# Seven quarter products in place of eight in the second feed-forward layer of a fused attention kernel

## The chip, the cores and the metric

The kernel runs on one core of a Trainium2 chip. The metric is the device time of one execution in microseconds (us), as the median of three runs. The core's engines work side by side, each through its own list of instructions in a fixed order, and wait for each other by semaphores. TensorE (PE in the profile) multiplies matrices into PSUM, eight banks of 128 x 512 float32. Its weight loads (PEld) overlap its matmuls. VectorE (DVE) and ScalarE (ACT) do elementwise work, GpSimd (POOL) sets up constants, and SyncE (SP) issues the DMA transfers between DRAM and SBUF.

## The reference

Attention over 4 batches, 8 heads, 576 tokens and width 64 gives `x` of 2304 tokens x 512. Two feed-forward layers follow, and the second one is what changes:

```python
# layer 1
h = x @ w_in                       # 2304 x 512 @ 512 x 2048
g = s * maximum(h, 0) ** 2 + b
x = g @ w_out                      # 2304 x 2048 @ 2048 x 512
# layer 2, with weights of its own
h = x @ w_in2
g = maximum(h, 0) + alpha * minimum(h, 0)
out = g @ w_out2
```

## The kernel before

**Precision.** Each operand of a large product is split into a high part, rounded to the type fp32r, and a low part, the difference. A product is then three matmuls: high by high, high by low and low by high. The weights arrive as 64-bit words and are put together from two 32-bit halves by three VectorE instructions (L870, L873, L876), then split by a cast (L879) and a difference (L882).

**Tiling.** Values lie transposed: features on the 128 partitions, tokens along the columns. Layer 1 runs over one block of 512 tokens and seven of 256, layer 2 over four of 512 and one of 256 (`BLOCKS`). In each block a loop over 16 slices `f` of the hidden width makes one step: `g1` runs the first product (4 slices of the input, 12 matmuls, L932 to L934) into a bank, ScalarE and VectorE make the hidden values from it and split them (in layer 1 relu L946, square L947, cast L954, difference L955; in layer 2 L949, L952, L954, L955), and `g2`, one step later, adds the second product (4 slices of the output, 12 matmuls, L973 to L975) into four banks. `evac` then copies the banks out (ScalarE L1003 or L1006, VectorE L1008 or L1012) and stores them, layer 1's to the DRAM tensor `y1`, layer 2's to the output. `load_x` loads a block of input and splits it (L1044 and L1046 in layer 1, L1051 and L1053 in layer 2).

**Order.** `op` records every instruction with its engine, an assumed duration, what it reads and writes, and a priority (a lower number goes first; without one, the place in the program). `Plan.order` then simulates all engines once, at build time, and writes out each engine's instructions in the order found. It includes SP's list of DMAs. At run time nothing is reordered: an instruction that waits holds up whatever is behind it on its engine. Temporary buffers are 19 slots of 640 columns, 12 in `pool` and 7 in `poolx`. A `Slot` takes a place when the plan reaches its first instruction, if as many places as its reserve (`RES`) stay free; `claim` closes places for good. The attention of all four batches comes first in priority, layer 1 fills in behind it, and layer 2's weights (`weights`, loaded by L867) are loaded and split from the attention's end on, most of them in layer 1's last block. The input of layer 1 goes through the DRAM tensor `x1` (stored by L833, loaded by L1035).

## Time and profile before

| | us |
|---|---|
| median of three runs | 980.5 |
| lowest and highest of them | 980.23, 982.16 |
| the profiled execution, its own time | 980.97 |
| its span in the profile, first to last instruction | 978.9 |

The profile is of one execution, taken by the hardware. Busy time is the time in which an engine had an instruction running. Matmuls are pipelined, so a row's duration is longer than the spacing of two matmuls, and the spacing has to be read from starts. A row of a group of instructions names line, engine, operation, output and inputs by their tiles, shape and count, then busy time in us, the mean duration of one in ns, and the engine's idle time just ahead of them with what ended it. A timeline row gives start and duration in us. The granted clock is the share of TensorE's full rate, 2.4 GHz, that it was given.

### The profile page before, as it was taken

Reading aid. Unit: us, or ns where it says so; the run is one execution under the profiler, and the core shown is the slowest. Engines: PE = TensorE matmul, PEld = TensorE weight load, DVE = VectorE, ACT = ScalarE, POOL = GpSimd, SP = SyncE. Lnnn points to the kernel's source line nnn. Section 1 sums busy time; section 2 is a strip of 40 time slices with the busy share of each in tenths; the row PEclk is TensorE's granted clock in tenths of the full one; section 3 lists DMA queues with packets and bytes.
Section 4 is the critical chain, followed back from the end, with each engine's and each line's share of the span. In section 5 each row is a group of like instructions: output and inputs, shape, how many; then the busy total and the mean of one; then the engine's idle time right before and its main releaser. Section 6 shows DMA issues by size and latency. Waiting matters only on the chain.

```text
span 978.9 us, 18001 instructions
## 1 busy us (share of the span) xinstructions
PE 962.6 (98%) x7068; PEld 828.7 (85%) x7068; DVE 602.4 (62%) x1471; ACT 471.5 (48%) x1183; POOL 5.3 (1%) x29
## 2 busy tenths in 40 slices
PE   7999999999999999999999999999999999999998
PEld 5777777788888888999999998888888888888898
DVE  7999998677776766542122999945434443534344
ACT  7877766787787777645454663212112111211111
POOL 1000000000000000000000000000000000000000
PEclk9999999999999999999999999999999999999999
DMA  5359955465657555641000755502000200100010
GB/s 176 100 161 239 243 197 155 111 163 115 151 117 155 137 121 104 120 164 55 1 23 10 224 170 158 162 1 86 1 1 11 65 1 1 44 1 0 1 45 22
DMA packets 114693, 93.22 MB, mean 95 GB/s; under 512 B 83377, under 2 KB 94641, under 8 KB 114609
## 3 DMA queue, kind: packets, MB, share of 16 engines
q1 hardware_dynamic: 114608, 92.08, 34.8%
q8 instruction: 55, 0.90, 0.4%
q14 instruction: 30, 0.24, 0.1%
HBM read 59.29 MB, written 13.11 MB: 74 GB/s over the span
## 4 chain that ended last, share of the span: by engine, by line
PE 89%; DVE 5%; ACT 4%; issue 1%; DMA 0%; SPq 0%; ACTq 0%; DVEq 0%
PE yb L973 13%; PE yb L975 13%; PE yb L974 13%; PE hb L932 9%; PE hb L934 8%; PE hb L933 8%; PE sp L932 3%; PE sp L934 3%; PE sp L933 3%; PE ob L775 2%; PE ob L932 2%; PE ob L934 2%; PE ob L933 2%; PE sp L775 2%; PE yb L775 2%; PE sp L679 1%
## 5 line engine op out<-in xcount | busy, mean ns | idle before, releaser
L973 PE MATMUL yb<-gr,wt 128*128 128x256 f32 (+2 forms) x832 | 270.7, 325 | 0.7 <-ACT gr L954 0.5
L975 PE MATMUL yb<-gr,wt 128*128 128x256 f32 (+2 forms) x832 | 268.3, 322 | 0.0
L974 PE MATMUL yb<-gr,wt 128*128 128x256 f32 (+2 forms) x832 | 267.6, 322 | 0.0
L932 PE MATMUL hb<-xr,wt 128*128 128x256 f32 (+1 forms) x592 | 183.9, 311 | 5.3 <-ACT gt L946 3.7
L934 PE MATMUL hb<-xr,wt 128*128 128x256 f32 (+1 forms) x592 | 179.1, 303 | 0.3 <-DVE wt L882 0.3
L933 PE MATMUL hb<-xr,wt 128*128 128x256 f32 (+1 forms) x592 | 179.1, 303 | 0.0
L973 PEld LDWEIGHTS yb<-gr,wt 128*128 128x128 f32 x832 | 156.4, 188 | 17.1 <-issue 2.5
L975 PEld LDWEIGHTS yb<-gr,wt 128*128 128x128 f32 x832 | 157.1, 189 | 13.9 <-DVE gr L955 1.1
L974 PEld LDWEIGHTS yb<-gr,wt 128*128 128x128 f32 x832 | 156.5, 188 | 12.2
L955 DVE TENSOR_TENSOR gr<-gt,gr 128x256 fp32r<-128x256 f32 (+1 forms) x168 | 84.1, 501 | 126.8 <-ACT gr L954 126.4
L954 ACT CAST gr<-gt 128x256 fp32r<-128x256 f32 (+1 forms) x168 | 78.7, 468 | 143.3 <-DVE gt L952 136.1
L932 PEld LDWEIGHTS hb<-xr,wt 128*128 128x128 f32 x592 | 111.3, 188 | 18.2 <-ACT gt L946 6.1
L934 PEld LDWEIGHTS hb<-xr,wt 128*128 128x128 f32 x592 | 111.8, 189 | 5.8 <-DVE wt L882 0.7
L933 PEld LDWEIGHTS hb<-xr,wt 128*128 128x128 f32 x592 | 111.3, 188 | 4.5
L946 ACT ACTIVATE gt<-hb 128x256 f32<-128x256 f32 (+1 forms) x128 | 52.6, 411 | 98.2 <-PE hb L934 94.1
L954 ACT CAST gr<-mz 128x512 fp32r<-128x512 f32 (+1 forms) x40 | 23.2, 579 | 154.0 <-DVE mz L952 153.9
L932 PE MATMUL sp<-xr,wt 128*128 128x512 f32 (+1 forms) x160 | 58.8, 367 | 0.0
L933 PE MATMUL sp<-xr,wt 128*128 128x512 f32 (+1 forms) x160 | 58.8, 367 | 0.0
L934 PE MATMUL sp<-xr,wt 128*128 128x512 f32 (+1 forms) x160 | 58.8, 367 | 0.0
L947 ACT ACTIVATE gt<-gt 128x256 f32<-128x256 f32 (+1 forms) x128 | 57.1, 446 | 2.5
L955 DVE TENSOR_TENSOR gr<-mz,gr 128x512 fp32r<-128x512 f32 (+1 forms) x40 | 25.6, 639 | 25.1 <-ACT gr L954 25.1
L949 DVE TENSOR_SCALAR mz<-ob,alv 128x512 f32<-128x512 f32 (+1 forms) x20 | 14.0, 698 | 37.8 <-PE ob L934 37.6
(343 smaller groups left out, 1484.7 us busy)
## 6 DMA issues: line engine op xcount, KB each, us to landing
pool<-wout SPq DMA_DIRECT2D x18, 512.0 KB, 4.3
pool<-win SPq DMA_DIRECT2D x16, 512.0 KB, 4.1
room<-wout SPq DMA_DIRECT2D x14, 512.0 KB, 3.9
room<-win SPq DMA_DIRECT2D x13, 512.0 KB, 4.2
pool<-y SPq DMA_DIRECT2D x18, 256.0 KB, 4.4
out_t<-pool SPq DMA_DIRECT2D x16, 256.0 KB, 2.1
y<-pool SPq DMA_DIRECT2D x22, 128.0 KB, 1.8
pool<-kp SPq DMA_DIRECT2D x9, 288.0 KB, 4.0
```

The costliest lines, as they stand in the source:

```text
L775: T.matmul(bank_at(bk)[rows, x:x + n], half(sqp, odd, q0, nq), half(sk, odd, k0, n), start=True, stop=True, skip_group_check=True)
L932: T.matmul(H_, W_h, X_h, start=(d == 0), stop=False)
L933: T.matmul(H_, W_h, X_l, start=False, stop=False)
L934: T.matmul(H_, W_l, X_h, start=False, stop=(d == KD - 1))
L946: op("ACT", t_act(n, 50), lambda: A.activation(out=t_, in_=H_, func=AF.Relu), r=[hk, "gr"], w=[tk], prio=-1)
L947: op("ACT", t_act(n), lambda: A.activation(out=t_, in_=t_, func=AF.Square), w=[tk], prio=-1)
L949: op("DVE", t_dve(n, 1.04, 60), lambda: V.tensor_scalar(out=t_, in0=H_, scalar1=0.0, scalar2=alv[:, f:f + 1], op0=ALU.min, op1=ALU.mult), ...
L954: op("ACT", t_act(n), lambda: A.copy(out=G_h, in_=t_), r=[tk], w=[("gh", gj)], prio=-1)
L955: op("DVE", t_dve(n), lambda: V.tensor_tensor(out=G_l, in0=t_, in1=G_h.bitcast(F32), op=ALU.subtract), r=[tk, ("gh", gj)], w=[("gl", gj)], ...
L973: T.matmul(Y, W_h, G_h, start=first, stop=False, skip_group_check=True)
L974: T.matmul(Y, W_l, G_h, start=False, stop=False, skip_group_check=True)
L975: T.matmul(Y, W_h, G_l, start=False, stop=False, skip_group_check=True)
```

## The change

Layer 1 stays as it is, except for where its tiles lie. Layer 2 no longer goes through `g1` and `g2`. Its input, its two weight matrices and its hidden values are each taken as 2 x 2 quarters (tokens by 1152, input width by 256, hidden width by 1024), and each product is made of seven products of sums and differences of quarters, numbered 1 to 7, whose results are added up to the four quarters of the output.

`prepare` loads the four quarters of a slice of layer 2's weights, puts the words together, forms the four sums and differences that the scheme needs, and stores all seven pieces in the DRAM tensors `wd`. `fetch` brings them back and splits them, into the places of layer 1's weights. `inputs` loads the input's quarters for 384 tokens of each half, adds layer 1's bias, and forms and splits the operands `XP` of the seven products. `hidden` runs the first product in 24 groups (3 passes over tokens by 8 slices of the hidden width), seven `product` calls of six matmuls each. Product 4 is run one group late. Partial results are kept in PSUM or copied out (`copy_out`), added up (`join`), put through the leaky relu (`leak`), and the hidden values are stored in the DRAM tensor `g1`. `output` loads them back by quarters, forms and splits operands in a ring of three buffers, runs the second product in 3 passes of seven products of four steps with 12 matmuls each, and stores the sums. All these matmuls have 384 columns.

```diff
-BLOCKS = {1: [(0, 512)] + [(t, 256) for t in range(512, NT, 256)],
-          2: [(t, min(512, NT - t)) for t in range(0, NT, 512)]}
+BLOCKS = [(0, 512)] + [(t, 256) for t in range(512, NT, 256)]
 NBIG, NB = 512, 256
+NS, NTH = 384, NT // 2
+GATE = 8
+GROUPS = [(b, f) for b in range(NTH // NS) for f in range(8)]
...
 def t_b(n):
...
         sb.tile([128, 16], F32, name="lead")
@@ -333,21 +341,29 @@
...
-            if layer == 1 and blk == len(BLOCKS[1]) - 1:
-                weights(win2, wout2, f, 2)
+            if blk == len(BLOCKS) - 1 and f % 2:
+                fetch("wi", f // 2)
...
+        PLACE = {1: (0, 0), 2: (0, 1), 5: (0, 2), 6: (0, 3), 3: (1, 0), 7: (1, 1), 4: (1, 2)}
...
+        def prepare(src, key, i):
...
+            fa, fb = Slot(RES["pf"], size=2), Slot(RES["pf"], size=2)
...
+            for x, f in enumerate((fa, fb)):
+                s = Slot(RES["pw"], size=2)
+                op("SP", 475, lambda s=s, x=x: nc.sync.dma_start(out=at(s, 1024, I32), in_=src[i, x]),
+                   r=[("x1", B - 1, NP - 1, 1), "words"], w=[s], bytes_=524288)
...
+            for out, in0, in1 in (((fa, 512), (fb, 0), (fa, 0)), ((fa, 768), (fb, 256), (fa, 512)),
+                                  ((fb, 512), (fb, 256), (fb, 0)), ((fb, 768), (fa, 256), (fa, 768))):
+                op("DVE", t_dve(256), lambda out=out, in0=in0, in1=in1: V.tensor_tensor(
+                    out=q(*out), in0=q(*in0), in1=q(*in1), op=ALU.subtract), r=[fa, fb], w=[out[0]])
+            for x, (f, a, n) in enumerate(((fa, 0, 4), (fb, 256, 3))):
+                op("SP", 475, lambda f=f, a=a, x=x, n=n: nc.sync.dma_start(
+                    out=wd[key][:, i, x, 0:256 * n], in_=q(f, a, 256 * n)), r=[f], w=[("wd", key, i, x)], bytes_=131072 * n)
+        def fetch(key, i):
...
+            for x, a, n in ((1, 0, 3), (0, 0, 2), (0, 2, 2)):
+                f = 2 * i + x
+                if key == "wi":
+                    old = wkeys("wi", f) + wkeys("wo", f)
+                    s = Buf("poolx", 2 * GW + (1024 if x else 256 * a), 256 * n)
+                else:
+                    old = []
+                    s = Buf("poolx", 0, 768) if x else Buf(4 + a // 2, 0, 512)
...
+                act(s, 475, lambda s=s, x=x, a=a, n=n: nc.sync.dma_start(out=see(s), in_=wd[key][:, i, x, 256 * a:256 * (a + n)]),
+                    r=[("wd", key, i, x)], extra_w=old, bytes_=131072 * n, prio=-4, eng="SP")
+                op("ACT", t_act(256 * n), lambda s=s, x=x, a=a, n=n: A.copy(out=wp(i, x)[:, a:a + n, 0, :], in_=fold(see(s))),
+                   r=s.keys, w=[("w2", i, x, a)], prio=-0.8 if key == "wi" else -0.5)
+                op("DVE", t_dve(256 * n), lambda s=s, x=x, a=a, n=n: V.tensor_tensor(
+                    out=wp(i, x)[:, a:a + n, 1, :], in0=fold(see(s)), in1=wp(i, x)[:, a:a + n, 0, :].bitcast(F32), op=ALU.subtract),
+                   r=s.keys, w=[("w2", i, x, a)], prio=-0.8 if key == "wi" else -0.5)
...
+        every = [("wd", key, i, x) for key in ("wi", "wo") for i in range(8) for x in range(2)]
+        def act(buf, dur, fn, r=(), prio=None, eng="ACT", extra_w=(), bytes_=0):
+            claim, extra = hold(buf)
+            op(eng, dur, fn, r=list(r) + (every if claim else []) + ([("g2", GATE)] if buf in XP.values() else []) + (
+                [("y1", len(BLOCKS) - 1, d) for d in range(KD)] if claim and max(claim) > NSLOT - XS + 4 else []),
+               w=buf.keys + extra + list(extra_w), prio=prio, claim=claim, bytes_=bytes_)
+        XP = {P: Buf("poolr", 4 * NS * i, 4 * NS) for i, P in enumerate((5, 6, 3, 2, 4))}
+        XP.update({P: Buf("xr", 4 * NS * i, 4 * NS) for i, P in enumerate((1, 7))})
+        RAW = [Buf("spare", 2 * NS * i, 2 * NS) for i in range(4)]
+        SUM = Buf("poolx", 0, 2 * NS)
+        FREE = [Buf(i, 0, NS) for i in range(6)]
...
+        def split(src, dst, prio):
+            act(dst, t_act(2 * NS), lambda: A.copy(out=see(dst, F32R, 0, 2 * NS), in_=see(src)), r=src.keys, prio=prio)
+            op("DVE", t_dve(2 * NS), lambda: V.tensor_tensor(
+                out=see(dst, F32R, 2 * NS, 2 * NS), in0=see(src), in1=see(dst, F32, 0, 2 * NS), op=ALU.subtract),
+               r=src.keys, w=dst.keys, prio=prio)
+        def sub(out, a, b, prio, o=ALU.subtract):
+            act(out, t_dve(out.n), lambda: V.tensor_tensor(out=see(out), in0=see(a), in1=see(b), op=o),
+                r=a.keys + b.keys, prio=prio, eng="DVE")
+        def inputs(b):
...
+            soon = -3 if b else -0.7
+            for P in (1, 5, 6, 3, 2, 7):
+                if P == 5:
+                    sub(SUM, a21, a22, soon, ALU.add)
+                elif P == 6:
+                    sub(SUM, SUM, a11, soon)
+                elif P == 3:
+                    sub(SUM, a12, SUM, soon)
+                elif P == 7:
+                    sub(a21, a11, a21, soon)
+                split({1: a11, 2: a12, 7: a21}.get(P, SUM), XP[P], soon)
+        def product(P, g, bank):
+            b, f = GROUPS[g]
+            def mm():
+                for k in range(2):
+                    X_h, X_l = (see(XP[P], F32R, 2 * NS * lo + NS * k, NS) for lo in range(2))
+                    W_h, W_l = (weight(P, f, lo, k) for lo in range(2))
+                    o = bank_of[bank][:, 0:NS]
+                    T.matmul(o, W_h, X_h, start=(k == 0 and P in (1, 5, 2)), stop=False, skip_group_check=True)
+                    T.matmul(o, W_h, X_l, start=False, stop=False, skip_group_check=True)
+                    T.matmul(o, W_l, X_h, start=False, stop=False, skip_group_check=True)
+            op("PE", t_s(NS), mm, r=[ready(P, f)] + XP[P].keys, w=[bank] + [("end", P)] * (g + 1 == len(GROUPS)), prio=MOE + cm["m"])
+            cm["m"] += 1
+        def copy_out(bank, out):
+            act(out, t_act(NS, 50), lambda: A.copy(out=see(out), in_=bank_of[bank][:, 0:NS]), r=[bank], prio=-1)
+        def join(bank, part, out):
+            act(out, t_dve(NS), lambda: V.tensor_tensor(out=see(out), in0=bank_of[bank][:, 0:NS], in1=see(part), op=ALU.add),
+                r=[bank] + part.keys, prio=-1, eng="DVE")
...
+        def leak(g, q, src, bank, out):
+            b, f = GROUPS[g]
+            f += 8 * (q % 2)
+            n = pick(TEMP)
+            r = [bank] if bank else src.keys
+            see_ = (lambda: bank_of[bank][:, 0:NS]) if bank else (lambda: see(src))
+            act(n, t_act(NS, 50 if bank else 93), lambda: A.activation(out=see(n), in_=see_(), func=AF.Relu, scale=-1.0), r=r, prio=-1)
+            act(out, t_dve(NS, 1.04, 60), lambda: V.scalar_tensor_tensor(
+                out=see(out), in0=see(n), scalar=alm[:, f:f + 1], in1=see_(), op0=ALU.mult, op1=ALU.add),
+                r=r + n.keys + ["alm"], prio=-1, eng="DVE")
+            k, t0 = GROUPS[g][1], NS * b
+            op("SP", 475, lambda: nc.sync.dma_start(out=g1_[:, q, k, t0:t0 + NS], in_=see(out)), r=out.keys,
+               w=[("g", b, q, k)], bytes_=512 * NS)
+        def hidden():
...
+            inputs(0)
+            ng = len(GROUPS)
+            bk = lambda g: (("S0", "H", ("Y", 0))[g % 3], ("O", ("Y", 2))[g % 2], ("S1", ("Y", 1))[g % 2])
+            parts = {}
+            def last(g):
+                al = bk(g)[0]
+                product(4, g, al)
+                leak(g, 2, None, al, pick(RING))
+                if GROUPS[g][0] == NTH // NS - 1:
+                    fetch("wo", GROUPS[g][1])
+            for g, (b, f) in enumerate(GROUPS):
+                al, be, ga = bk(g)
+                p1, u2, p5 = (SIDE[3 * (g % 2) + x] for x in range(3))
+                product(1, g, al)
+                copy_out(al, p1)
+                product(5, g, ga)
+                copy_out(ga, p5)
+                if g > 0:
+                    last(g - 1)
+                if f == 0:
+                    split(RAW[3], XP[4], -3 if b else -0.7)
+                product(6, g, al)
+                copy_out(al, u2)
+                product(3, g, ga)
+                c = pick(RING)
+                join(ga, u2, c)
+                leak(g, 1, c, None, c)
+                product(2, g, be)
+                c = pick(RING)
+                join(be, p1, c)
+                leak(g, 0, c, None, c)
+                product(7, g, al)
+                c = pick(RING)
+                join(al, p5, c)
+                leak(g, 3, c, None, c)
+                if f == 7 and g + 1 < ng:
+                    inputs(b + 1)
+            last(ng - 1)
...
+        def output():
+            U = [quarter(q) for q in range(4)]
+            ring = [Buf("gr", 0, 4 * NS)] + [Buf("xr", 4 * NS * i, 4 * NS) for i in range(2)]
+            side = FREE + [Buf("poolx", 4 * NS + NS * i, NS) for i in range(7)] + SIDE[0:3]
...
+                t0 = NS * b
+                for q in (3, 2, 0, 1):
+                    for m in range(4):
+                        act(U[q][m], 475, lambda u=U[q][m], q=q, m=m, t0=t0: nc.sync.dma_start(
+                            out=see(u).rearrange("p (k n) -> p k n", k=2), in_=g1_[:, q, 2 * m:2 * m + 2, t0:t0 + NS]),
+                            r=[("g", b, q, 2 * m + e) for e in range(2)] + (
+                                [("end", P) for P in (5, 6, 3, 2, 4)] if U[q][m].region == "poolu" else []), eng="SP", bytes_=1024 * NS)
+                kept = {}
+                for P in (4, 5, 1, 2, 6, 3, 7):
+                    bank = names[{1: "a", 6: "a", 7: "a", 2: "b", 5: "c", 3: "c", 4: "d"}[P]]
+                    for m in range(4):
+                        a11, a12, a21, a22 = (U[q][m] for q in range(4))
+                        if P == 5:
+                            sub(a22, a21, a22, None, ALU.add)
+                        elif P == 6:
+                            sub(a22, a22, a11, None)
+                        elif P == 3:
+                            sub(a12, a12, a22, None)
+                        elif P == 7:
+                            sub(a21, a11, a21, None)
+                        src = {4: a22, 5: a22, 6: a22, 1: a11, 2: a12, 3: a12, 7: a21}[P]
+                        dst = ring[count[0] % len(ring)]
+                        count[0] += 1
+                        split(src, dst, None)
+                        def mm(P=P, m=m, dst=dst, bank=bank):
+                            for e in range(2):
+                                G_h, G_l = (see(dst, F32R, 2 * NS * lo + NS * e, NS) for lo in range(2))
+                                for j in range(2):
+                                    W_h, W_l = (weight(P, 2 * m + e, lo, j) for lo in range(2))
+                                    o = bank_of[bank[j]][:, 0:NS]
+                                    T.matmul(o, W_h, G_h, start=(m == e == 0 and P in (1, 2, 4, 5)), stop=False, skip_group_check=True)
+                                    T.matmul(o, W_l, G_h, start=False, stop=False, skip_group_check=True)
+                                    T.matmul(o, W_h, G_l, start=False, stop=False, skip_group_check=True)
+                        op("PE", 2 * t_s(NS), mm, r=[ready(P, 2 * m + e) for e in range(2)] + dst.keys, w=bank,
+                           prio=MOE + cm["m"])
+                        cm["m"] += 1
+                    for j in range(2):
+                        if P in (4, 5, 1, 6):
+                            kept[P, j] = buf()
+                            copy_out(bank[j], kept[P, j])
+                        else:
+                            for part, q in {2: ((1, 0),), 3: ((6, 1),), 7: ((4, 2), (5, 3))}[P]:
+                                c = buf()
+                                join(bank[j], kept[part, j], c)
+                                d, tq = j + 2 * (q % 2), t0 + NTH * (q // 2)
+                                op("SP", 475, lambda c=c, d=d, tq=tq: nc.sync.dma_start(out=outT[:, d, tq:tq + NS], in_=see(c)),
+                                   r=c.keys, bytes_=512 * NS)
-        for i, (layer, blk) in enumerate((l, j) for l in (1, 2) for j in range(len(BLOCKS[l]))):
-            moe(layer, blk, i % 2 if layer == 1 else 2 + blk % 2)
+        for key, src in (("wi", win2), ("wo", wout2)):
+            for i in range(8):
+                prepare(src, key, i)
+        for blk in range(len(BLOCKS)):
+            moe(blk, blk % 2)
         flush()
+        hidden()
+        output()
```

Left out of the diff are the buffers' bookkeeping (`Buf`, `see`, `hold`), the loads of the input with its bias, the places of the quarters in `output`, the new layout of the weights' array, and the lines of layer 1 that only lose their layer argument.

## Rows read from the trace of the kernel before

**Rows 1.** Page, busy time (share of the span) and instructions of each engine

```profile
PE 962.6 (98%) x7068; PEld 828.7 (85%) x7068; DVE 602.4 (62%) x1471; ACT 471.5 (48%) x1183; POOL 5.3 (1%) x29
```

**Rows 2.** Page, TensorE's busy tenths and granted clock in 40 slices of the span

```profile
PE   7999999999999999999999999999999999999998
PEclk9999999999999999999999999999999999999999
```

**Rows 3.** Windows: us; busy (count) of PE, PEld, DVE, ACT, POOL; clock, DMA share, GB/s

```profile
450.00:500.00 50.00, 50.00 (x438) 49.80 (x437) 10.50 (x26) 24.43 (x64) 0.00 (x0) 1.00 0.08 25
550.00:600.00 50.00, 50.00 (x353) 46.92 (x352) 47.86 (x88) 26.58 (x58) 0.00 (x0) 1.00 0.62 182
700.00:750.00 50.00, 50.00 (x222) 41.40 (x221) 19.21 (x27) 5.61 (x9) 0.00 (x0) 1.00 0.00 1
```

**Rows 4.** Timeline of VectorE, layer 2's 512-wide blocks: first and last of 25 L949

```profile
684.81 0.75 DVE L949 TENSOR_SCALAR mz<-ob,alv 128x512 f32<-128x512 f32 x1 [2.51 <-PE ob L934]
...
815.37 0.75 DVE L949 TENSOR_SCALAR mz<-ob,alv 128x512 f32<-128x512 f32 x1 [2.50 <-PE ob L934]
```

**Rows 5.** Timeline: first and last of 12 L955, 12 L955 (258 wide), 15 L949

```profile
458.83 0.43 DVE L955 TENSOR_TENSOR gr<-gt,gr 128x256 fp32r<-128x256 f32 x1 [2.29 <-ACT gr L954]
...
488.75 0.43 DVE L955 TENSOR_TENSOR gr<-gt,gr 128x256 fp32r<-128x256 f32 x1 [2.29 <-ACT gr L954]
...
503.04 0.43 DVE L955 TENSOR_TENSOR gr<-gt,gr 128x256 fp32r<-128x256 f32 x1 [2.39 <-ACT gr L954]
...
533.99 0.43 DVE L955 TENSOR_TENSOR gr<-gt,gr 128x256 fp32r<-128x256 f32 x1 [2.39 <-ACT gr L954]
...
932.43 0.48 DVE L949 TENSOR_SCALAR mz<-sp,alv 128x256 f32<-128x256 f32 x1 [0.72 <-PE sp L934]
...
972.01 0.49 DVE L949 TENSOR_SCALAR mz<-ob,alv 128x256 f32<-128x256 f32 x1 [0.91 <-PE ob L934]
```

**Rows 6.** Groups of instructions by line and form, the two widths of cast and difference

```profile
L955 DVE TENSOR_TENSOR gr<-gt,gr 128x256 fp32r<-128x256 f32 x120 | 50.9, 424 | 106.8 <-ACT gr L954 106.4
L954 ACT CAST gr<-gt 128x256 fp32r<-128x256 f32 x120 | 48.8, 406 | 19.5 <-DVE gt L952 16.9 <-PE yb L974 0.2
L955 DVE TENSOR_TENSOR gr<-gt,gr 128x512 fp32r<-128x512 f32 x48 | 33.2, 691 | 20.0 <-ACT gr L954 20.0
L954 ACT CAST gr<-gt 128x512 fp32r<-128x512 f32 x48 | 29.9, 623 | 123.8 <-DVE gt L952 119.1 <-PE yb L974 3.7 <-PE yb L975 1.0
```

**Rows 7.** Timeline of VectorE without gaps, 256 and 512 wide

```profile
546.69 0.42 DVE L955 TENSOR_TENSOR gr<-gt,gr 128x256 fp32r<-128x256 f32 x1
547.03 0.42 DVE L870 TENSOR_SCALAR pool<-pool 128x512 int32<-128x512 int32 x1
547.37 0.68 DVE L882 TENSOR_TENSOR wt<-pool,wt 128x512 fp32r<-128x512 f32 x1
547.97 0.68 DVE L873 SCALAR_TENSOR_TENSOR pool<-pool 128x512 int32<-128x512 int32 x1
```

**Rows 8.** Timeline of SP: last x1 store, weight loads, last y1 stores

```profile
422.26 0.32 SPq L833 DMA_DIRECT2D x<-pool  x1
...
425.37 0.41 SPq L867 DMA_DIRECT2D pool<-win  x1
425.87 0.38 SPq L867 DMA_DIRECT2D pool<-wout  x1
...
584.97 2.04 SPq L1014 DMA_DIRECT2D y<-pool  x4
```

**Rows 9.** DMA issues from 424.5 to 426.5: KB each, us from issue to landing

```profile
pool<-win SPq DMA_DIRECT2D x1, 512.0 KB, 4.0
pool<-wout SPq DMA_DIRECT2D x1, 512.0 KB, 5.2
```

**Rows 10.** Timeline of the end: last matmul, last copy out of a bank

```profile
975.13 0.28 PE L975 MATMUL yb<-gr,wt 128*128 128x256 f32 x1
...
975.44 0.43 DVE L1012 COPY pool<-yb 128x256 f32<-128x256 f32 x1 [0.25 <-PE yb L975]
```

More of the change, by code (lines that the diff above doesn't have):

```diff
@@ L978, in g2 @@
                    w=[yk, ("g2", f)] + ([(yslot[d], "y")] if d in yslot else []),
[L979 removed]
+                   prio=MOE + cm["m"] + (1.5 if n == NBIG else 0))
             cm["m"] += 1
@@ L1035, in load_x @@
                 op("SP", 475, lambda xr=xr, src=src: nc.sync.dma_start(out=xr(), in_=src), r=rk,
-                   w=[s] + [("xset", x) for x in ((0, 1, 3) if xs == 3 else (xs,))], bytes_=512 * step * n,
-                   prio=-2 if layer == 2 and blk > 0 else None)
+                   w=[s, ("xset", xs)], bytes_=512 * step * n)
                 for e in range(step):
@@ new lines, in ready, with weight, __init__ @@
+        def ready(P, i):
+            x, a = PLACE[P]
+            return ("w2", i, x, 0 if x else a // 2 * 2)
+        def weight(P, i, lo, k):
+            x, a = PLACE[P]
+            return wp(i, x)[:, a, lo, k * 128:(k + 1) * 128]
+        class Buf:
+            def __init__(self, region, c0, n):
+                self.region, self.c0, self.n = region, c0, n
+                key = "pool" if region in ("poolr", "poolu") else region
+                self.keys = [(key, c) for c in range(c0 // 128, (c0 + n + 127) // 128)]
@@ new lines, in build, with hold @@
+        seen = set()
+        def hold(buf):
+            claim, extra = [], []
+            for k in buf.keys:
+                if k in seen:
+                    continue
+                seen.add(k)
+                region, c = k
+                lo, hi = 128 * c, 128 * c + 127
+                if region == "pool":
+                    claim += range(NSLOT - XS)
+                elif region == "poolx":
+                    o = NSLOT - XS
+                    claim += range(o + lo // GW, o + hi // GW + 1)
+                elif region == "xr":
+                    extra += [("xset", int(hi >= 2 * KD * NB))]
+                elif isinstance(region, int):
+                    extra += wkeys("wi", 2 * region + 1) + wkeys("wo", 2 * region + 1)
+                elif region in ("gr", "gt"):
+                    extra += [(x, j) for x in (("gh", "gl") if region == "gr" else ("gt",)) for j in range(2)]
+            return sorted(set(claim)), list(dict.fromkeys(extra))
```

260 lines of the change are left out of this document (142 added, 118 removed).

## The prediction

> **What bounds the kernel now.** I read the busy times first, then the slices of the span, then the stages in windows, and last the rows from which one instruction is priced. TensorE is busy 962.6 of 978.9 us, the next engine 602.4 [rows 1]; its busy digit is 9 from the second of the forty slices to the last but one [rows 2]. In the windows of layer 1 and layer 2 it is busy for the whole 50 us, with VectorE at 10 to 20 us of 50, except where layer 2's weights are decoded, 47.86 of 50 [rows 3]. So what layer 2 costs is its matmuls times their spacing, and only taking matmul time away, or adding waits, moves the end.
>
> The spacing has to be read from a marker that comes once in each step of 24 matmuls (12 of the first product, 12 of the second), because a busy matmul row overlaps its neighbours and some records are missing. In the 512-wide blocks 24 steps lie between 684.81 and 815.37 [rows 4]: 5.44 us a step, 226.7 ns a matmul. In the 256-wide block at the end 14 steps take 39.58 us [rows 5]: 2.827 us, 117.8 ns. Layer 2 is therefore 4 x 16 x 5.44 + 16 x 2.827 = 348.2 + 45.2 = 393.4 us, nothing idle in it. Layer 1's 256-wide blocks give 2.72 us (11 steps in 29.92), 113.3 ns, and the block with 258 columns in its second product 2.814 us (11 steps in 30.95): with 113.3 ns for its 12 matmuls of 256 columns, the 258-wide ones take 121 ns [rows 5].
>
> **The change: what leaves TensorE.** Seven quarter products in place of eight. First product: 24 groups x 7 x 6 = 1008 matmuls; second: 3 passes x 7 x 4 x 12 = 1008; all 384 wide, 2016 of them in place of 1536 of 512 and 384 of 256. No row has 384 columns. In cycles of 2.4 GHz (the granted clock is 1.00 throughout, its upper level [rows 2]) 256 columns cost 272, 258 cost 291 and 512 cost 544: 16 over the columns at 256, 32 or 33 above. So I take 384 + 32 = 416, 173.3 ns. The bounds are the ratio of the clean rows, 17/16, 170.0 ns, and that of the slower last block, 117.8 x 1.5 = 176.7 ns. Then 2016 x 173.3 = 349.4 us (342.7 to 356.2), and TensorE loses 393.4 - 349.4 = 44.0 us (37.2 to 50.7). Instructions grow from 1920 to 2016, so not the whole eighth comes back.
>
> The Trainium skill, TensorE: Matmul & The Clock Gate, section "Wait — 56ns, not 53.3ns?", puts a warm stream at the columns over 2.4 plus about 2.5 ns, 215.7 ns measured at 512. The rows say 226.7 ns [rows 4] and decide. By the page, as an estimate, layer 2 would be 373.4 before and 327.6 after, 45.8 us less.
>
> **What is added beside TensorE, and its cover.** The prices: a VectorE instruction on 256 columns starts 0.34 us before the next, one on 512 columns 0.60 [rows 7]; along that line 384 columns are 0.47 and 768 are 0.86 (the profile's durations, 424 and 691 ns, contain a tail under the next instruction [rows 6]). ScalarE casts take 406 and 623 ns [rows 6], so 0.51 and 0.84.
> - First product, per group of 42 matmuls = 7.28 us: VectorE three joins and four leaks, 7 x 0.47 = 3.3 us; ScalarE three copies and four relus, 3.6 us. Covered. Each value TensorE waits for (a copy out of a bank before the next product adds to it) has two other products, 2.08 us, between, against 0.51 plus handing over.
> - A new pass over 384 tokens: 11 more VectorE instructions of 0.86 (9.5 us) and ScalarE 7 x 0.84 + 8 x 0.51 = 10.0 us, within about two groups (14.6 us) that hold 6.6 already: 16.1 in 14.6. The operands are single buffers, each free only after its last product in group 7 and wanted one group later. TensorE waits 0 to 4 us there; I take 1.0 for each of two.
> - Second product, per pass 28 x 12 x 173.3 = 58.2 us: VectorE 44 x 0.86 + 8 x 0.47 = 41.6, ScalarE 28 x 0.84 + 8 x 0.51 = 27.6. The products 6, 3 and 7 are the dense part: 12 steps of 1.72 plus two joins, 21.6 in 25 us. Covered by a ring of three buffers, 0 to 2 us a pass; I take 0.5 x 3.
> - Weights: decoding them was 32 x (0.34 + 3 x 0.60) = 68.5 us of VectorE; now 32 x 1.54 + 64 x 0.34 = 71.1 us, moved ahead to the time after the attention, and 16 x (0.86 + 2 x 0.60) = 33.0 us for fetching and splitting again, half of it in layer 1's last block, half in the last pass of the first product. VectorE has the room: 10.5 of 50 us in layer 1's middle [rows 3].
>
> **Waits that the change adds.** (1) The loads of one pair of weight pieces wait until the pair before is decoded. Behind them on SP stand layer 1's stores and loads; behind each decode that waits for its load stands, on VectorE, the low part of the hidden values, for which the next second product waits. Two such loads issued 0.5 us apart landed after 4.0 and 5.2 us [rows 8, 9], so the second is there at 5.7; decoding 1.54 and handing over make 7.5 us a pair, 16 pairs 120 us. The attention's last store is issued at 422.3 and the first load then at 425.4 [rows 8]: done near 546, the last pieces stored near 551. The operand buffers in the pool want all of them, and step 8 of layer 1's last block, seven steps of 2.827 before the last stores at 585.0 [rows 8], near 565. So 14 us of slack. VectorE's order is fixed ahead, so loads later than planned can hold TensorE: 0 to 10 us, I take 1.5. (2) Layer 2's first operands can be split only after step 8: 6 splits and 4 differences of 0.86, four weight fetches of 2.06 and layer 1's own 7 x 0.34 are 19.2 us of VectorE in the 20 that are left, but product 1 needs only the first split: 0 to 8 us, I take 2.0. (3) Between the two products, the loads of three of the four quarters wait for the last product 4, whose operands stood in their place. Only product 4 (four steps of 2.08 = 8.3 us) runs without them. A load of 0.39 MB lands 4.0 us after issue and each next one 1.3 later (0.39/0.52 of the 1.7 us between the two landings above); sum, cast and difference take 2.6: 6.6 us, just within the cover; 0 to 7, I take 1.0. (4) At the end four joins follow the last matmul where four copies, two of them on ScalarE, did: the last one started 0.31 us after the last matmul's start [rows 10]. Two joins more in VectorE's row are 0.94 us, of which a half-step is hidden: 0.5 (0 to 1.5).
>
> Sum of the waits: 2 x 1.0 + 1.5 + 1.5 + 2.0 + 1.0 + 0.5 = 8.5 us. The profiled execution took 980.97 us, 2.07 over its span, and the median of the runs is 980.5, 0.5 lower: 980.97 - 44.0 + 8.5 = 945.5, and 945.0 for a median.
>
> **Rivals.**
> - Spacing at the ratio 17/16 and next to no waits: 980.5 - 50.7 + 1 = 931. For it: both clean rows have that ratio. Against: 258 columns already pay what 512 pay [rows 5].
> - Layer 2 starts late or layer 1 is paced by weight loads: the two upper bounds, 10 and 8 for 3.5, give 945 + 14.5 = 959.5. For: both engines' rows in that block come to nine tenths of it. Against: the 14 us of slack.
> - The second product is paced by its chain: if the difference of the next step isn't run under the cast, a step takes 0.86 + 0.84 + 0.86 = 2.56 where TensorE wants 2.08; 48 steps (four products of four, three passes) x 0.48 = 23 us, 968; with handing over of 0.25 each, 980, no change. Against: the ring holds three steps and the order is planned ahead.
> - Slower: the pool gives no room for two pairs of weights in flight, so each pair also waits for the stores of the one before: 5.7 + 1.54 + four differences of 0.34 + 4.0 for the stores, with handing over about 13 us, 16 pairs 208 us, until 633; layer 2 can run only product 1 before, 48 us after layer 1's end: 993 to 1001. It decides from 10 us a pair on. For: the stores use the same queue. Against: a pair wants 8 of 19 slots.
> - Slower: the clock falls at each new wait. One group at half the rate costs 7.28 us more; at six places (start, two passes, the boundary, two passes) 44 us, 989. Against: the granted clock is 1.00 in all forty slices although TensorE idled 16 us of the span [rows 1, 2]. The same page of the Trainium skill, section "HAM oscillation — how this bites in real kernels", says that idling brings the lower level back; no run here shows it.
>
> **How the numbers follow.** Forecast, 933 to 955 (the small waits at their ends and the spacing between its bounds): 0.66. Close spacing, 925 to 933: 0.08. Late start, 955 to 966: 0.11. Chain in the second product: 0.07, of which 0.02 at no change. Weights too slow: 0.06. Clock: 0.02. From 931 to 966 lies about 0.83. Faster by over 0.2% (2 us, what a measurement of this kernel can tell): 0.66 + 0.08 + 0.11 + 0.05 = 0.90; same 0.02; slower 0.08.
>
> **What would show it.** Right: markers of the first product's groups 7.2 to 7.4 us apart and steps of the second near 2.08; TensorE busy to the end with idle time of some 8 us after 420, at the four places named; granted clock 1.00. Wrong: groups of 7.5 us or more (spacing), decodes that wait for loads with TensorE's gaps right behind (weights), TensorE waiting for VectorE in products 6, 3 and 7 (chain), or a gap of several microseconds between the two products (the quarters' loads).

## The result, and the profile after

The changed kernel takes 955.5 us (median of four runs, 954.75 to 957.7) against 980.9 for the kernel before (four runs as well): a ratio of 0.9743, 95% interval 0.9723 to 0.9763, 25.5 us less. Forecast were 945.0, between 931 and 966, faster with 0.9. The direction and the range hold; of the 36 us that were expected to remain, 10 are missing. All rows of after in this section are from a run of 957.7 us with a span of 955.8.

Page, busy time of each engine, and TensorE's busy tenths and granted clock in 40 slices, to be read beside [rows 1, 2]:

```profile
PE 926.7 (97%) x7164; PEld 849.3 (89%) x7164; DVE 720.9 (75%) x1638; ACT 605.4 (63%) x1411; POOL 5.4 (1%) x29
...
PE   7989999999999899999999999799999999999998
PEclk9899999999999999999999999899999999999999
```

TensorE still sets the time. Its instructions are 96 more, as counted ahead, and it is busy 36 us less. Two slices of the clock are now below 9, the second and the 26th (597 to 621 us), and in the latter the busy digit falls to 7 as well: that is layer 2's start. What the second slice costs is settled with e9. Windows of 100, 25 and 200 us (columns as in [rows 3]):

```profile
300.00:400.00 100.00, 96.95 (x1046) 84.70 (x1042) 67.83 (x219) 75.75 (x208) 1.03 (x5) 0.98 0.60 131
...
600.00:625.00 25.00, 17.91 (x79) 16.14 (x78) 17.11 (x29) 13.66 (x26) 0.00 (x0) 0.80 0.63 201
...
725.00:925.00 200.00, 200.00 (x1150) 198.98 (x1150) 162.12 (x216) 107.16 (x169) 0.00 (x0) 1.00 0.55 170
```

From 725 to 925, which holds the change from the first product to the second, no time is lost, while VectorE is busy four fifths of it. From 600 to 625, 79 matmuls stand where 144 would fit. Between 300 and 400, in the attention, 3 us are idle; before it was less than 1. The spacing of the new matmuls, timeline of TensorE, six steps from one row to the other:

```profile
589.50 0.33 PE L1233 MATMUL ob<-poolr,wp 128*128 128x384 f32 x1
...
590.54 0.33 PE L1233 MATMUL sp<-xr,wp 128*128 128x384 f32 x1
```

1.04 us for six is 173.3 ns, 416 cycles of 2.4 GHz: the forecast's value. What TensorE waits for (waits by engine and line: us in total, times, longest) has entries that the kernel before has not:

```profile
PE sp L1233 <- DVE poolx L1260: 5.6, 1, 5.6
...
PE hb L925 <- ACT xr L1018: 1.6, 1, 1.6
PE hb L1233 <- DVE poolx L1248: 1.2, 1, 1.2
```

The first of them, in the timelines of TensorE, ScalarE, VectorE and SP:

```profile
610.74 0.34 PE L1235 MATMUL ob<-poolr,wp 128*128 128x384 f32 x1
616.70 0.69 PE L1233 MATMUL sp<-xr,wp 128*128 128x384 f32 x1 [5.62 <-DVE poolx L1260]
617.19 0.52 PE L1234 MATMUL sp<-xr,wp 128*128 128x384 f32 x1
617.51 0.52 PE L1235 MATMUL sp<-xr,wp 128*128 128x384 f32 x1
...
612.70 0.83 ACT L1107 CAST wp<-poolx 128x768 fp32r<-128x768 f32 x1 [1.93 <-DMA poolx<-wdwi]
...
613.56 2.43 DVE L1109 TENSOR_TENSOR wp<-poolx,wp 128x768 fp32r<-128x768 f32 x3 [2.07 <-ACT wp L1107]
616.03 0.61 DVE L1260 SCALAR_TENSOR_TENSOR poolx<-poolx,alm,sp 128x384 f32<-128x384 f32 x1
...
609.26 6.45 SPq L1105 DMA_DIRECT2D poolx<-wdwi  x5
```

TensorE wants a PSUM bank (sp) for a new product 1. The bank is held by a finished product 4 until its leak (L1260) has read it, and the leak stands behind the weights' differences (L1109), which wait for their casts (L1107), which wait for the weights to land (L1105). Why a leak should come after the weights is in the plan of places: `RING`, the buffers for the leak's output, lies with four of its seven buffers on columns 1280 to 2816 of poolx, and `fetch` puts the weights on 1280 to 3072 of the same tile until the last slice is through.

Behind the wait the matmuls stand 0.32 us apart. The granted clock in three stretches:

```profile
612.00:616.00 4.00, 0.00 (x0) 0.00 (x0) 2.29 (x3) 2.07 (x3) 0.00 (x0) 0.89 0.56 147
616.00:624.00 8.00, 6.06 (x18) 5.55 (x19) 5.68 (x10) 3.94 (x8) 0.00 (x0) 0.50 0.28 104
624.00:626.00 2.00, 2.00 (x10) 2.00 (x9) 1.76 (x4) 1.83 (x5) 0.00 (x0) 0.66 0.92 331
```

It fell to 0.50, the 1.2 GHz level, while TensorE stood still, and was back about 9 us after the matmuls had begun again. The 65 matmuls that are missing from 600 to 625 are 65 x 0.1733 = 11.3 us; 7.1 of them are idle time (25.00 - 17.91), so some 4 us, by this estimate, are the slower spacing. The prediction could cite the Trainium skill's section "HAM oscillation — how this bites in real kernels" (TensorE: Matmul & The Clock Gate), that idling brings the lower level back, without a row for it; this trace agrees, 0.50 after 5.62 us.

In the attention, SP's rows (the last x1 store answers to [rows 8], where it is at 422.26 us) show a thing of layer 2 that is there early, two of its loads of y1:

```profile
185.40 2.04 SPq L1205 DMA_DIRECT2D spare<-y  x2
...
425.74 0.32 SPq L851 DMA_DIRECT2D x<-pool  x1
```

And the end, last matmul and the joins behind it, to be read beside [rows 10]:

```profile
950.84 0.34 PE L1365 MATMUL sp<-xr,wp 128*128 128x384 f32 x1
...
950.69 1.02 DVE L1248 TENSOR_TENSOR gr<-sp,waste 128x384 f32<-128x384 f32 x2 [4.07 <-PE sp L1365]
951.63 0.55 DVE L1248 TENSOR_TENSOR gt<-sp,waste 128x384 f32<-128x384 f32 x1
952.09 0.55 DVE L1248 TENSOR_TENSOR waste<-sp,waste 128x384 f32<-128x384 f32 x1
```

The span ends 4.96 us after the last matmul's start (955.8 - 950.84), before 3.77 (978.9 - 975.13).

The theory from this trace: 44 us came, as computed; about 9 went at layer 2's start (the wait, and the clock that fell with it), about 7 in the attention, whose work is in another order, and 1.2 at the end. The program makes the order of all engines' work with a planner, so an instruction that layer 2 adds can move others far ahead of it. The first such instruction in VectorE's list is a 90-ns operation (`alm` from `alv`, L1270), which needs only what is there from the start.

All runs, each against runs of the kernel before on the same chip:

| Kernel | us | ratio to before, 95% interval |
|---|---|---|
| after | 955.5 | 0.9743 (0.9723 to 0.9763) |
| e1: layer 2 kept out of the attention | 956.3 | 0.9757 (0.9741 to 0.9773) |
| e2: other buffers for the leak | 946.8 | 0.9651 (0.9628 to 0.9673) |
| e3: both | 940.6 | 0.9592 (0.9578 to 0.9606) |
| e4: before, one 90-ns operation more | 996.9 | 1.0170 (1.0155 to 1.0185) |
| e5: the wait filled with matmuls | 955.6 | 0.9737 (0.9716 to 0.9757) |
| e6: e3, product 3 last | 939.2 | 0.9574 (0.9558 to 0.9590) |
| e7: e4 without moving the weights | 981.9 | 1.0014 (1.0001 to 1.0026) |
| e8: e3, weights moved by 64 bytes | 950.8 | 0.9688 (0.9668 to 0.9708) |
| e9: e3, the operation free | 941.5 | 0.9590 (0.9574 to 0.9606) |
| e10: e3, the loads free | 950.7 | 0.9686 (0.9672 to 0.9700) |

### The profile page after: what moved, and what is told of

It is laid out like the page before. It is cut to its first block, busy times and chain, and to the rows that moved or that the text cites. A ratio compares the mean times of both kernels' runs of the same rounds, so it can differ in the third digit from the quotient of the medians.

```text
span 955.8 us, 19300 instructions
## 1 busy us (share of the span) xinstructions
PE 926.7 (97%) x7164; PEld 849.3 (89%) x7164; DVE 720.9 (75%) x1638; ACT 605.4 (63%) x1411; POOL 5.4 (1%) x29
## 4 chain that ended last, share of the span: by engine, by line
PE 88%; DVE 4%; ACT 4%; DMA 3%; issue 1%; SPq 0%; DVEq 0%
PE hb L925 7%; PE yb L959 7%; PE hb L926 7%; PE yb L961 7%; PE hb L927 7%; PE yb L960 6%; PE yb L1363 3%; PE yb L1365 3%; PE yb L1364 3%; PE sp L1363 3%; PE sp L1365 3%; PE sp L1364 3%; PE sp L793 2%; PE yb L1233 2%; PE yb L1235 2%; PE yb L1234 2%
## 5 line engine op out<-in xcount | busy, mean ns | idle before, releaser
L925 PE MATMUL hb<-xr,wt 128*128 128x256 f32 (+1 forms) x512 | 153.3, 299 | 4.5 <-ACT gt L938 2.8
L959 PE MATMUL yb<-gr,wt 128*128 128x256 f32 (+2 forms) x512 | 153.4, 300 | 0.5 <-ACT gr L940 0.5
L961 PE MATMUL yb<-gr,wt 128*128 128x256 f32 (+2 forms) x512 | 150.3, 293 | 0.4 <-DVE gr L941 0.4
L926 PE MATMUL hb<-xr,wt 128*128 128x256 f32 (+1 forms) x512 | 149.5, 292 | 0.2 <-DVE xr L1020 0.2
L927 PE MATMUL hb<-xr,wt 128*128 128x256 f32 (+1 forms) x512 | 149.4, 292 | 0.0
L925 PEld LDWEIGHTS hb<-xr,wt 128*128 128x128 f32 x512 | 96.6, 189 | 10.9 <-ACT gt L938 4.3
L959 PEld LDWEIGHTS yb<-gr,wt 128*128 128x128 f32 x512 | 96.5, 188 | 9.7 <-issue 5.9
L941 DVE TENSOR_TENSOR gr<-gt,gr 128x256 fp32r<-128x256 f32 (+1 forms) x128 | 58.4, 456 | 59.1 <-ACT gr L940 57.2
L961 PEld LDWEIGHTS yb<-gr,wt 128*128 128x128 f32 x512 | 96.4, 188 | 3.7 <-DVE gr L941 1.0
L927 PEld LDWEIGHTS hb<-xr,wt 128*128 128x128 f32 x512 | 96.4, 188 | 2.7
L926 PEld LDWEIGHTS hb<-xr,wt 128*128 128x128 f32 x512 | 96.4, 188 | 2.6 <-DVE xr L1020 0.4
L960 PE MATMUL yb<-gr,wt 128*128 128x256 f32 (+2 forms) x320 | 93.5, 292 | 0.0
L960 PEld LDWEIGHTS yb<-gr,wt 128*128 128x128 f32 x320 | 60.2, 188 | 1.3
L960 PE MATMUL yb<-gr,wu 128*128 128x256 f32 (+2 forms) x192 | 56.1, 292 | 0.0
L1259 ACT ACTIVATE waste<-poolx 128x384 f32<-128x384 f32 x48 | 25.2, 525 | 25.9 <-DVE poolx L1248 25.7
L1190 ACT CAST xr<-spare 128x768 fp32r<-128x768 f32 x30 | 25.0, 835 | 25.0 <-PE sp L1364 7.5
L960 PEld LDWEIGHTS yb<-gr,wu 128*128 128x128 f32 x192 | 36.1, 188 | 0.7
L1233 PE MATMUL yb<-poolr,wp 128*128 128x384 f32 x104 | 35.7, 343 | 0.0
```

The costliest lines, as they stand in the source:

```text
L925: T.matmul(H_, W_h, X_h, start=(d == 0), stop=False)
L926: T.matmul(H_, W_h, X_l, start=False, stop=False)
L927: T.matmul(H_, W_l, X_h, start=False, stop=(d == KD - 1))
L941: op("DVE", t_dve(n), lambda: V.tensor_tensor(out=G_l, in0=t_, in1=G_h.bitcast(F32), op=ALU.subtract), r=[tk, ("gh", gj)], w=[("gl", gj)], ...
L959: T.matmul(Y, W_h, G_h, start=first, stop=False, skip_group_check=True)
L960: T.matmul(Y, W_l, G_h, start=False, stop=False, skip_group_check=True)
```

## The experiments

Differences in us below are differences of these ratios times 980.9.

**e2, the leak's buffers.** For the first eight groups, the ring uses buffers off the fetch's place:

```
-RING = [Buf("poolx", 5 * GW + NS * i, NS) for i in range(3)] + [Buf("poolx", 2 * GW + NS * i, NS) for i in range(4)]
+RING = [Buf("poolx", 5 * GW + NS * i, NS) for i in range(3)] + FREE[4:6]
...
+if g == 8:
+    RING[:] = [Buf("poolx", 5 * GW + NS * i, NS) for i in range(3)] + [Buf("poolx", 2 * GW + NS * i, NS) for i in range(4)]
```

> The kernel after, but in layer 2's first pass the leak's output goes round five buffers that lie clear of the place through which the weights are fetched, instead of seven, four of which lie on it. Theory (the 5.6 us wait on the buffer is the cause, and the clock's fall follows from the wait): the wait goes, the granted clock stays at 0.95 or above between 600 and 626 us, and the matmuls of 384 columns stand 0.173 us apart from the start: 9 us less, 946. Rival (the clock falls at the change of layers whatever the wait): only the wait goes, 5 to 6 us less, 950, and the clock is still near 0.5 for some microseconds. Rival (the real limit is the fetch of weights, and the wait only showed on the buffer): the wait moves to the products' weights, 954 to 956.

Measured: 9.0 us less than after (0.9743 - 0.9651; by the two intervals some 3 us either way). The windows that answer to those of after:

```profile
612.00:616.00 4.00, 4.00 (x25) 4.00 (x24) 4.00 (x8) 3.77 (x8) 0.00 (x0) 1.00 0.97 341
616.00:624.00 8.00, 7.86 (x44) 7.22 (x43) 7.17 (x14) 5.24 (x12) 0.00 (x0) 1.00 0.80 240
```

TensorE is busy where it stood, and the clock is 1.00. So the wait was on the shared place, not on the weights, which still come through the same three staging pieces; and the stall's price was the wait and the slow stretch together.

**e1, layer 2 kept out of the attention.** Without e2's edit:

```
 op("DVE", 90, ... out=alm, in0=alv ...
-   r=["alv"], w=["alm"])
+   r=["alv", ("x1", B - 1, NP - 1, 1)], w=["alm"])
...
-rk = [("y1", j, d0 + e) ...
+rk = [("x1", B - 1, NP - 1, 1)] + [("y1", j, d0 + e) ...
```

> The kernel after, but the 90-ns VectorE operation on alv and the first loads of y1 for layer 2 wait for the last x1 store, so that nothing of layer 2 is in the attention's order of work. Theory (a new order of the attention costs 7 us): the last x1 store is issued at 422 us again (425.7 after) and layer 1's last y1 store at 585 (597 after); about 948 us if the stall at layer 2's start stays at 9 us. Rival (the attention's delay is not from the order, but from load of memory or queues by layer 2's preparation): the last x1 store stays at 425 to 426 and the time at 955. A third reading, from the schedule that the program computes: the attention is quicker but the stall at layer 2's start grows from about 9 to 16 us, since the weights' fetch does not move forward with it: 953 to 957, with a larger wait on the leak's buffer.

Measured: as after (0.9757, the intervals overlap). The last x1 store is issued at 421.5, so the attention is quick again, but the start of layer 2 takes it back (the longest wait of TensorE, and the window):

```profile
PE hb L1233 <- DVE poolx L1248: 11.6, 1, 11.6
PE ob L1233 <- ACT wp L1107: 2.5, 1, 2.5
...
600.00:625.00 25.00, 10.59 (x36) 9.75 (x36) 13.55 (x21) 10.39 (x18) 0.00 (x0) 0.66 0.55 179
```

The third reading held: what is won ahead of a wait whose end is set elsewhere only makes the wait longer.

**e3, both edits.**

> The edits of e1 and e2 together. Theory: 7 us and 9 us add up: 939 to 941 us, the last x1 store at 422, no wait over 1 us at layer 2's start. If the attention's delay is not from the order, 946 as e2. If the wait only moves, 948 or more.

Measured: 940.6, 5.8 us under e2 (0.9651 - 0.9592) and 40.0 under the kernel before. The two losses add up once the wait is gone. Its attention in the window that answers to the one of after has the kernel before's values:

```profile
300.00:400.00 100.00, 99.16 (x1074) 89.14 (x1074) 69.01 (x219) 77.41 (x218) 1.02 (x5) 1.00 0.58 131
```

**e4 and e7, the 90-ns operation alone.** e4 adds to the kernel before:

```
+alm = sb.tile([128, KF], F32, name="alm")
...
+op("DVE", 90, lambda: V.tensor_scalar(out=alm, in0=alv, scalar1=-1.0, scalar2=1.0, op0=ALU.mult, op1=ALU.add),
+   r=["alv"], w=["alm"])
```

> The kernel before, with nothing added but the 90-ns VectorE operation on alv (its output is not used). Theory (that one operation in VectorE's order makes the program choose another order for all of the attention, and that order is slower): the last x1 store at 425 to 426 us, the whole 985 to 988 us, 5 to 7 us over the kernel before. Rival (the attention's delay comes from layer 2's other work): within 0.2% of the kernel before, 979 to 983 us, the last x1 store at 422.

Measured: 16.7 us slower, far over both. Only part of the surplus is in the attention: the last x1 store is at 426.0, 3.8 us later than before, layer 1's last y1 stores at 591.65, 6.7 later than in [rows 8]. The largest part, some 8 of the 14.9 us between the two profiles' spans (993.8 - 978.9), is in layer 2, whose code is untouched: 433 of its matmuls stand in 100 us where 443 stood, with nothing idle. The new tile had moved weights' tiles by 64 bytes in SBUF, those of twelve of the sixteen slices; the program places the tiles of the last four (`room`) ahead of the new one. VectorE's marker (L950 here) shows both spacings in layer 2, in two steps near the end of one block and in eight of the next:

```profile
660.69 0.75 DVE L950 TENSOR_SCALAR mz<-sp,alv 128x512 f32<-128x512 f32 x1 [2.62 <-PE sp L935]
...
671.57 0.75 DVE L950 TENSOR_SCALAR mz<-ob,alv 128x512 f32<-128x512 f32 x1 [2.51 <-PE ob L935]
...
693.84 0.75 DVE L950 TENSOR_SCALAR mz<-ob,alv 128x512 f32<-128x512 f32 x1 [2.67 <-PE ob L935]
...
738.64 0.75 DVE L950 TENSOR_SCALAR mz<-ob,alv 128x512 f32<-128x512 f32 x1 [2.67 <-PE ob L935]
```

5.44 us a step, as in [rows 4], where the weights hadn't moved, and 5.60, 233.3 ns a matmul, where they had. e7 makes the same operation write into an unused stretch:

```
-sb.tile([128, TAIL], F32, name="tail")
+alm = sb.tile([128, TAIL], F32, name="tail")[:, 0:KF]
```

> The kernel before with only the 90-ns operation on alv added, as e4, but its output goes into an unused stretch of SBUF instead of a tile of its own, so that the weights' tiles stay where they were (e4 moved them by 64 bytes). Theory (e4's 16 us are two things: a slower order of the attention, 4 to 7 us, and a slower spacing of layer 2's matmuls, 233 instead of 227 ns for 512 columns, by the weights' place, 9 to 10 us): spacing 227 ns again, 985 to 988 us, the last x1 store at 425 to 426. Rival (the spacing came with the order of work): spacing 233 ns, 996. Rival (the order alone costs nothing): 980 to 981.

Measured: 1.4 us over before (1.0014), 15 under e4. The windows of e4 and of e7:

```profile
800.00:900.00 100.00, 100.00 (x433) 80.99 (x432) 40.84 (x61) 13.85 (x24) 0.00 (x0) 1.00 0.03 11
```
```profile
800.00:900.00 100.00, 100.00 (x443) 82.81 (x442) 42.55 (x62) 13.87 (x24) 0.00 (x0) 1.00 0.03 11
```

So 15 us of e4's surplus were the weights' place, and the operation costs 1.4 us (0.1 to 2.6 by the interval) and not the 4 to 7 that I had set. The order of the attention does change (last x1 store at 423.8), but this change of it is cheap. My culprit falls.

**e9 and e10, which of layer 2's early things it is.** e9 is e3 without the edit on `alm`, e10 is e3 without the edit on the loads.

> As e3, but of the two things of layer 2 that e3 holds back until the last x1 store, only the loads of y1 are held; the 90-ns VectorE operation is free to stand in the attention. Theory (the operation alone costs the 1.4 us that it cost in the kernel before, the loads' place in the order the other 5): 941.5 to 943. Rival (the operation is the whole cause): 946 to 948, as e2.

> As e3, but only the 90-ns VectorE operation is held back until the last x1 store; the loads of y1 for layer 2 may be issued as soon as their block of layer 1 is stored. Theory (the loads cost about 5 us by the order of work): 945 to 946.5, with TensorE idle some 5 us more between 180 and 430 us than in e3. Rival (they cost nothing): 940 to 941.5. The schedule that the program computes for itself is 10 us longer with these loads free, so 950 is possible too.

Measured: e9 equals e3 (0.9590 and 0.9592); e10 is 9.2 us slower (0.9686). It is the loads of y1. The operation shows only at the attention's start: in the first 50 us of e9 the granted clock is 0.97 (1.00 in e3), a dip as in the second slice of after, and the whole is no longer for it. In e10, as in after, the loads begin in the attention, at 182.4 us. Two windows, TensorE's longest wait, and the chain that ends it (rows of SP, ScalarE and TensorE) are:

```profile
200.00:300.00 100.00, 100.00 (x1056) 88.64 (x1055) 69.41 (x228) 79.68 (x219) 0.82 (x4) 1.00 0.60 136
300.00:400.00 100.00, 93.46 (x968) 81.29 (x967) 64.96 (x213) 70.84 (x200) 0.82 (x4) 0.95 0.57 123
...
PE hb L925 <- ACT xr L1018: 3.5, 1, 3.5
...
329.06 0.37 SPq L1011 DMA_DIRECT2D pool<-x  x1
...
332.33 0.71 ACT L1018 CAST xr<-pool 128x256 fp32r<-128x256 f32 x2 [4.30 <-DMA pool<-x]
...
332.79 0.58 PE L925 MATMUL hb<-xr,wt 128*128 128x256 f32 x1 [3.48 <-ACT xr L1018]
```

L1018 is the cast of layer 1's input; the same wait is 1.6 us in after and absent between 300 and 400 in e3. Nothing uses the loaded values before 544 us. That the early loads cost 6 us (e2 against e9) to 9 (e10 against e3) is shown. Their own transfers don't do it: the two are issued at 182.4 and 190.2 us and land some 4 us later, TensorE is busy the whole time from 200 to 300, and the stall comes at 329, with a granted clock of 0.50 from 331 to 340 us behind it. The order does differ there: in e3 SP issues three loads of layer 1's input (L1011) at 322.35 to 323.80, ahead of the y1 stores from 331.57 on; in e10 it issues one at 320.45, then four y1 stores, and the two others at 329.06 and 329.52. That this order, which the planner gives once it has the loads, is the cause fits all these rows; no run changes it alone.

**e5, the wait filled.** Before group 3's product 1, in the kernel after; each `extra` is six matmuls of product 1's operands into a bank that the first product doesn't use:

```
+if g == 3:
+    for x in range(5):
+        extra(g)
 product(1, g, al)
```

> The kernel after, and 30 more matmuls of 384 columns (5.2 us of TensorE, their sums go into a PSUM bank that nothing reads there) in the place of the 5.6 us wait at layer 2's start; the wait itself stays as long as it was. Theory (the clock falls because TensorE stands idle): the granted clock stays at 0.95 or above from 600 to 626 us, the matmuls behind stand 0.173 us apart, and the kernel is 3 to 4 us quicker than after though it does more work: 951 to 952.5. Rival (the clock falls for another reason at the change of layers): still 0.5 for some microseconds, and 955 to 956 us. Against the kernel before: 0.970 to 0.972 by the theory, 0.974 to 0.975 by the rival.

Measured: 955.6, no gain. TensorE's waits, and the clock behind them:

```profile
PE hb L1233 <- DVE poolx L1258: 2.1, 1, 2.1
PE sp L1233 <- DVE poolx L1270: 1.4, 1, 1.4
...
618.00:622.00 4.00, 3.09 (x10) 3.09 (x11) 3.80 (x8) 2.27 (x6) 0.00 (x0) 0.57 0.03 6
```

(L1258 and L1270 are L1248 and L1260 of after.) The 5.6 us shrank to 1.4, but 2.1 remained one product further, behind the same chain, and the clock fell again, for some 3 us in place of 10. The expectation took one wait for the whole chain. The run doesn't separate the wait's price from the clock's; e2 shows their sum only, and the split of 7.1 and 4 us above is an estimate.

**e6, the order at the end.**

```
-for P in (4, 5, 1, 2, 6, 3, 7):
+for P in (4, 5, 1, 2, 6, 7, 3) if t0 + NS == NTH else (4, 5, 1, 2, 6, 3, 7):
```

> The edits of e3, and in the last pass of the output product 7 (four additions behind it) comes before product 3 (two additions behind it). Theory (the additions behind the last matmul are the tail, 0.46 to 0.5 us each on VectorE): the time from the last matmul to the end falls from 5.0 to about 4.0 us, 939 to 940. Rival (the tail is the last store's transfer): as e3, 940.6.

Measured: 939.2 (0.9574). The last matmul and the last joins:

```profile
933.58 0.34 PE L1367 MATMUL yb<-xr,wp 128*128 128x384 f32 x1
...
933.96 0.56 DVE L1248 TENSOR_TENSOR waste<-yb,poolx 128x384 f32<-128x384 f32 x1
```

The last join now starts 0.38 us behind the last matmul, 1.25 in after, and the span ends 3.8 us behind it (937.4 - 933.58). The trace shows the 1.1 us; the ratios' intervals for e3 and e6 overlap. This is the quickest version, 41.8 us under the kernel before.

**e8, the weights' place under layer 2's new matmuls.** `TAIL = 40` becomes 24 in e3: an unused stretch before the weights is 64 bytes shorter, which moves the tiles of the same twelve slices.

> The edits of e3, and the weights' tiles moved by 64 bytes in SBUF (16 words less of an unused stretch before them). Theory (the place of the weights against that of the moving values sets the spacing): the matmuls of 384 columns stand further apart than 0.1733 us, near 0.180 if the 6.6 ns that e4 showed at 512 columns come with every matmul; 2016 of them and layer 1's give 10 to 20 us, 951 to 961. Rival (the place matters only at 512 columns, or not at all): 940 to 942.

Measured: 950.8, 9.4 us over e3 (0.9688 - 0.9592). But the 384-wide matmuls keep their spacing but for a third of a per cent (577 of them between 800 and 900 us, 579 in e3). Layer 1's 256-wide blocks lose it: its last y1 stores are issued at 594.85, 586.99 in e3, 7.9 of the 9.4 us. VectorE's timeline, the marker that comes once in 24 matmuls, over four steps of e3 and three of e8:

```profile
464.00 0.43 DVE L941 TENSOR_TENSOR gr<-gt,gr 128x256 fp32r<-128x256 f32 x1 [1.62 <-ACT gr L940]
...
474.88 0.43 DVE L941 TENSOR_TENSOR gr<-gt,gr 128x256 fp32r<-128x256 f32 x1 [0.50 <-ACT gr L940]
```
```profile
463.74 0.43 DVE L941 TENSOR_TENSOR gr<-gt,gr 128x256 fp32r<-128x256 f32 x1 [0.31 <-ACT gr L940]
...
472.38 0.43 DVE L941 TENSOR_TENSOR gr<-gt,gr 128x256 fp32r<-128x256 f32 x1 [0.66 <-ACT gr L940]
```

2.72 us a step against 2.88, 113.3 and 120.0 ns a matmul. The theory was right that the place counts and wrong about where: not in the 384-wide matmuls.

## Why the prediction was right, and where its steps failed

What leaves TensorE came as computed. That the time still lies in the range is in part luck: its upper part was there for late operands, slow weight loads and waits at four places, and it was filled by two losses that came by ways the sum did not have. TensorE's waits from 425 us on add up to 8.4 us, near the 8 of the prediction's signs, but 7.1 of them lie at one place, and the granted clock did not stay at 1.00.

- **What leaves TensorE, -44.0 us:** right. 173.3 ns is measured, 416 cycles as taken from 544 at 512 columns. e3, without the two large losses, is 40.0 us under the kernel before, which is 44.0 less a tail of 1.2, a pass hand-over of 0.5 and a start that still idles 1.3 of 25 us, within 1 us.
- **Pass hand-overs, 2 x 1.0:** 0.5 in all; the longest one is 0.47 us.
- **Second product's chain, 1.5, and the boundary, 1.0:** nothing; TensorE is busy 200.00 of 200 us. Product 4 covered the loads of the three other quarters, as worked out, and the values' way through DRAM cost nothing there. The chain-paced rival is out.
- **(1) Weights in layer 1, 1.5:** nothing. The sixteen pairs took longer than the 7.5 us each that I had set: the last store is issued at 566.6 us, not near 551, and the slack of 14 us was used up. But TensorE waits 0.9 us in all between 425 and 600, and layer 1's steps are 2.72 us as in [rows 5]. The rival with serial stores is out.
- **(2) Layer 2's start, 2.0 with a bound of 8:** the failed step, 9.0 us by e2 (some 3 either way). I counted VectorE's work in that block (19.2 of 20 us) and asked when the first operands are ready. They were ready in time. What I didn't ask is where each output goes: the leak writes into a buffer on the fetch's place, and through it a PSUM bank and TensorE hang on the last weight slice. The price of such a wait was also set without the clock, which I had put into a rival of its own at 0.02; it fell at one of that rival's six places.
- **(4) The tail, 0.5 (to 1.5):** 1.2, mis-sized: both added joins are exposed, 0.46 us each, 0.9 of the 1.2, and none is hidden under a half-step.
- **Left out: the attention,** 5.8 us by e3 against e2. I took everything ahead of 422 us as fixed since no instruction there was edited. But layer 2's first loads of y1 may go as soon as layer 1 has stored their block, which is at 185 us, and with them the work there runs in another order, in which TensorE waits and the clock falls (0.98 from 300 to 400 us in after, 0.95 in e10). The sum had no term for it.

The sum with the measured terms: -44.0 + 0.5 + 9.0 + 1.2 + 5.8 = -27.5, against -25.5 measured; 2 us, about the width of the two ratios' intervals that the terms rest on, aren't assigned.

## What to carry to other kernels

When a change moves values into buffers that something else also passes through, list for each output which earlier user must be done with its place, and follow it back to the engine that sets the time; counting an engine's work is not enough. Where a program chooses its order by itself, every new instruction that may start early is part of the change from that moment on: hold it back to where it is wanted, and look whether the stretch before is as it was. And after adding a tile, see whether others moved: it can cost more than the edit.

## What the runs showed of the hardware that was not expected

- 64 bytes of place in SBUF are worth up to 6% of a matmul's spacing. With the weights of twelve of the sixteen slices moved and the values that stream past them left where they were, 256-wide matmuls went from 113.3 to 120.0 ns (e8) and 512-wide ones from 226.7 to 233.3 (e4), at a granted clock of 1.00; 384-wide ones stayed at 173 ns. The Trainium skill, SBUF — State Buffer, section "Who interferes with whom", gives TensorE's weights and moving values a read port each and names only the port pair of VectorE and GpSimd as a place of contention; these runs show a slower stream that this rule has no place for. The place isn't all of it: layer 1's last block, with its tiles in the same places, takes three steps in 8.16 us in after (first two rows), 2.72 each, and in 8.48 in e3, 2.83 each. What else counts, and whether it is the width or the other tiles that spares the 384-wide matmuls, stays open.

```profile
561.26 0.43 DVE L941 TENSOR_TENSOR gr<-gt,gr 128x256 fp32r<-128x256 f32 x1 [1.96 <-ACT gr L940]
...
569.42 0.43 DVE L941 TENSOR_TENSOR gr<-gt,gr 128x256 fp32r<-128x256 f32 x1 [2.29 <-ACT gr L940]
```
```profile
559.39 0.42 DVE L941 TENSOR_TENSOR gr<-gt,gr 128x256 fp32r<-128x256 f32 x1 [1.73 <-ACT gr L940]
...
567.87 0.42 DVE L941 TENSOR_TENSOR gr<-gt,gr 128x256 fp32r<-128x256 f32 x1 [1.39 <-ACT gr L940]
```

- The clock's fall needn't follow one long wait. In e5 TensorE stood for 1.4 and 2.1 us with six matmuls between, and the clock was 0.57 from 618 to 622 us, the stretch that begins in the second wait. In the attention of after it was 0.53 from 335 to 338.6 us, behind waits of 0.70 and 1.63 us.
